# A state-space layer and a gated long convolution on one core: the same 815 operations in another order string

## The chip, the cores and the metric

The kernel runs on one core of a Trainium2 chip. The metric is the device time of one execution in microseconds (us); lower is better. TensorE is PE (its weight loads are PEld), VectorE is DVE, ScalarE is ACT, GpSimd is POOL, SyncE is SP; SPq and ACTq are the queues on which SP and ACT issue transfers.

## The reference, cut to what matters

There are two parts, each on a sequence of 2048 positions with 640 channels, and their outputs stand side by side.

```
A:  Bu   = x @ B_bar.T            (complex, 640 states)
    h_t  = Lam_bar * h_(t-1) + Bu_t
    y    = 2 * Re(h @ C.T) + x * Dskip
B:  kv   = (causal 4-tap convolution of k, by channel) * v
    y    = irfft(rfft(kv padded) * rfft(ssm_k padded))[:2048] + kv * ssm_D
    out  = q * y
result = concat([A, B], axis=-1)          # bf16, 1 x 2048 x 1280
```

## The kernel before, in words

Everything lives in one SBUF tensor (`arena`) and one PSUM tensor of eight banks (`acc`). The function `build` (it calls the methods of `PartA` and `PartB`) adds 815 small operations to a list with `P.add`. An operation has a number, a name, the engines that could run it, a function that makes its instructions, and its footprints. `depend` works out from the footprints which operation must wait for which. The string `ORDER` then says everything else: each entry is an operation's number, the letter of its engine (T PE, V DVE, A ACT, G POOL, S SP) and the first PSUM bank of its group. A small t is PE with the narrow tile form: the product is cut into two halves of the array (`wide`, L225 wide and L229 narrow; `s1`, L876 wide and L881 narrow). `emit` walks the string and makes the instructions, so each engine runs its entries in that order, and an entry that waits holds up all behind it on its engine. There is no planner in the file; only its result.

Operations of part A, in the order of the data: `warm` (L539, products that only keep PE busy at the start); `ld_Braw`, `turn_B`, `ev_B` (L517 to L526: B loaded, transposed on PE, copied out) and `ld_B2` (L512, the rest of B by transposing transfers); `ld_x` (L547, x by eight transposing transfers); `up2`, `up1`, `up0a`, `up0b`, `up0c` (L581 and L602, with evictions L598, L622, L648), a tree that combines neighbouring positions with the tables `rr` (L457, four of them, numbers 143 to 146, products on DVE); `coarse` (`cs_v`, `cs_m`, `cs_s` and so on, L666 to L690), the scan over the top of the tree in two halves, whose scratch is the buffer H0; `dn3` to `dn0` with `ad` (L225/L229 and L728), the way back down; `gm` (L457) and `gC` (L571, L575), C scaled; and `project` (L736 to L765): `ld_r`, `xd` (x times Dskip, L737), `C0` to `C15` (20 or 40 products each, L225/L229), `ev_C` (L754 on DVE, or L752 on ACT with `em_C`, L760, after it) and the store `st_A`.

Operations of part B: five blocks of 128 channels go through `ld_k`, `ld_v` (L814, transposing transfers), the convolution (`cm`, four taps, L205 on DVE and L206 on ACT; `ca`, three adds, L840; `cx`, times v, L841), a store to DRAM (`pl`, L847) and eight loads per half in another layout (`rl`, L857). There is one buffer for k, so `ld_k` of a block waits for all taps of the block before it. Two halves of the channels are then transformed: `s1` and `s2` for h (the filter, `ld_h`, L807, into H0) and for k (L876/L881 with evictions L886, and L900 with evictions L913), the complex products `pp`, `pq`, `py`, `pz` (L924 to L931), the way back `r2` (L951, L956) and `r1` (L972; L990 on DVE, or L988 on ACT and then `em1`, L995), and the stores (L1006). `c.DR` is the Dskip row spread over the partitions (`ld_Dr`, number 91, L372); `ld_D` (157 and 158, L795) are two loads of 640 bytes.

Every PSUM group takes two banks as a rule, and the group that follows on the same banks waits for the eviction of the one before. SP issues nearly all transfers, in the order of its entries.

```
order = [(int(x[:-2]), x[-2].upper(), int(x[-1])) for x in ORDER.split()] if ORDER else plain_order(c.P)
c.P.narrow = {int(x[:-2]) for x in ORDER.split() if x[-2] == "t"}
```

Of the kernel before, what the change touches and what calls it, by code (L numbers as in the profile page):

```python
# [1097 lines left out]
def plain_order(P):  # L1098
# [16 lines left out]


ORDER = (
# [40 lines left out]
)  # L1158


# [68 lines left out]
```

## Time and profile before

| what | value |
|---|---|
| median of three runs | 188.85 us (188.34 to 191.32) |
| span of the profiled execution, first to last instruction | 187.3 us |
| what lies between that span and the runs' median | 1.55 us |
| PE, DVE, ACT, POOL busy | 175.6, 158.0, 147.7, 72.6 us |
| transfers | 30.15 MB, 161 GB/s over the span |
| granted TensorE clock, mean | 0.999 |

The profiled execution's own time is known as its span; the runs' times are of whole executions. Instruction rows are start, length, engine, line, operation, output and inputs, and in brackets how long the engine idled before it and what ended that. PE's busy time counts pipelined products whose ends are modelled, so a high share is not a full array. A transfer's row on SPq is the time that its issue took, not the transfer's.

### The profile page before, as it was taken

The page shows a single profiled execution, that of the slowest core. Times are in us where ns is not written, and L with a number is a line of the kernel's source. Part 1 is how long each engine was busy: PE and PEld are TensorE (multiplying, and loading weights), DVE is VectorE, ACT ScalarE, POOL GpSimd, SP SyncE. Part 2 cuts the span into 40 slices and gives each one's busy share as a digit, 9 for nine tenths or more (in the row PEclk, how much of TensorE's full clock was granted, in tenths as well). Part 3 has the DMA queues.
Part 4 walks back from the last instruction along what each step waited for, and adds up shares of the span by engine and source line. Part 5 has one row for each costly group of instructions (what it writes and reads, how often), then busy time and mean ns, then how long its engine had stood idle before and what let it go on. Part 6 is the DMA issues. An engine that isn't in the chain of part 4 may idle for free.

```text
span 187.3 us, 7665 instructions
## 1 busy us (share of the span) xinstructions
PE 175.6 (94%) x3398; PEld 126.3 (67%) x3399; DVE 158.0 (84%) x225; ACT 147.7 (79%) x181; POOL 72.6 (39%) x68
## 2 busy tenths in 40 slices
PE   7998999999799979979997999999999999999992
PEld 2565666677468756656685688776588876887770
DVE  3537964679959899999969999899999999998961
ACT  2469699989899979999997997997898883985000
POOL 8679999900000000008803925730740000551620
PEclk9999999999999999999999999999999999999999
DMA  5999999799999989999989479402496993058996
GB/s 153 191 184 158 200 143 140 141 174 182 198 253 154 290 179 152 180 182 154 138 109 251 154 170 133 75 5 72 122 196 120 210 227 85 15 160 187 208 219 173
DMA packets 106682, 30.15 MB, mean 161 GB/s; under 512 B 101274, under 2 KB 106010, under 8 KB 106650
## 3 DMA queue, kind: packets, MB, share of 16 engines
q1 hardware_dynamic: 106332, 29.35, 86.7%
q8 instruction: 26, 0.43, 1.1%
q10 hardware_dynamic: 318, 0.33, 0.6%
q14 instruction: 6, 0.05, 0.1%
HBM read 11.32 MB, written 7.86 MB: 102 GB/s over the span
## 4 chain that ended last, share of the span: by engine, by line
PE 54%; DVE 23%; DMA 9%; ACT 8%; issue 3%; DVEq 0%; ACTq 0%
PE acc L225 17%; PE acc L581 13%; DMA arena<-in_B_k_dram 9%; PE acc L229 6%; DVE arena L728 6%; PE acc L900 6%; DVE arena L205 5%; ACT arena L913 5%; PE acc L951 4%; DVE arena L840 3%; PE acc L972 3%; PE acc L539 2%; DVE arena L754 2%; PE acc L881 1%; ACT arena L886 1%
## 5 line engine op out<-in xcount | busy, mean ns | idle before, releaser
L581 PE MATMUL acc<-arena 128*64 128x512 bf16 x400 | 45.6, 380 | 1.8 <-DVE arena L457 1.1
L913 ACT CAST arena<-acc 128x960 bf16<-128x960 f32 (+1 forms) x43 | 37.4, 916 | 4.0 <-PE acc L900 2.2
L225 PE MATMUL acc<-arena 128*128 128x320 bf16 (+2 forms) x255 | 36.4, 297 | 2.2 <-DVE arena L754 1.1
L581 PEld LDWEIGHTS <-arena 128*64 128x64 bf16 x400 | 26.0, 110 | 17.8 <-DVE arena L457 1.3
L886 ACT CAST arena<-acc 128x1024 bf16<-128x1024 f32 x37 | 35.8, 1034 | 2.1 <-PE acc L881 2.0
L225 PEld LDWEIGHTS <-arena 128*128 128x128 bf16 x256 | 23.7, 98 | 12.1 <-DVE arena L754 1.3
L841 POOL TENSOR_TENSOR arena<-arena 128x2048 bf16<-128x2048 bf16 x2 | 8.8, 4410 | 53.7 <-DVE arena L840 46.1
L900 PE MATMUL acc<-arena 128*64 128x160 bf16 x512 | 23.6, 235 | 1.8 <-DVE arena L679 1.4
L900 PEld LDWEIGHTS <-arena 128*64 128x64 bf16 x512 | 18.6, 110 | 8.3 <-ACT arena L913 2.2
L229 PE MATMUL acc<-arena 128*64 128x320 bf16 (+3 forms) x258 | 23.2, 313 | 0.5 <-DVE arena L690 0.5
L840 DVE TENSOR_TENSOR arena<-arena 128x2048 bf16<-128x2048 bf16 x14 | 17.6, 1256 | 4.5 <-ACT arena L206 4.3
L728 DVE TENSOR_TENSOR arena<-acc,arena 128x1024 bf16<-128x1024 f32 (+2 forms) x19 | 20.4, 1114 | 0.9 <-PE acc L229 0.5
L760 POOL TENSOR_TENSOR arena<-arena 128x640 bf16<-128x640 f32 x3 | 4.2, 1416 | 32.6 <-ACT arena L752 32.6
L956 ACT CAST arena<-acc 128x1024 bf16<-128x1024 f32 x16 | 15.4, 1025 | 1.7 <-PE acc L951 1.6
L229 PEld LDWEIGHTS <-arena 128*64 128x64 bf16 x258 | 13.0, 110 | 3.5 <-DVE arena L690 0.6
L876 PE MATMUL acc<-arena 128*64 128x128 bf16 x400 | 14.6, 220 | 0.2 <-ACT arena L886 0.2
L876 PEld LDWEIGHTS <-arena 128*64 128x64 bf16 x400 | 12.9, 110 | 2.4 <-ACT arena L886 0.9
L205 DVE TENSOR_SCALAR arena<-arena 128x2048 bf16<-128x2048 bf16 x15 | 11.0, 749 | 3.6 <-DMA arena<-in_B_k_dram 3.5
L754 DVE TENSOR_TENSOR arena<-acc,arena 128x640 bf16<-128x640 f32 x13 | 10.7, 820 | 3.5 <-PE acc L225 2.2
L206 ACT ACTIVATE arena<-arena 128x2048 bf16<-128x2048 bf16 (+2 forms) x10 | 11.1, 1112 | 1.5 <-DMA arena<-in_B_k_dram 1.5
L924 DVE TENSOR_TENSOR arena<-arena 128x2560 bf16<-128x2560 bf16 x8 | 11.9, 1484 | 0.1
L602 PE MATMUL acc<-arena 128*64 128x256 bf16 (+2 forms) x140 | 11.6, 291 | 0.1
(142 smaller groups left out, 284.4 us busy)
## 6 DMA issues: line engine op xcount, KB each, us to landing
out_dram<-arena SPq DMA_DIRECT2D x32, 160.0 KB, 3.3
arena<-in_B_ssm_k_dram SPq DMA_DIRECT2D x8, 320.0 KB, 6.1
kv_rows<-arena SPq DMA_DIRECT2D x5, 512.0 KB, 4.7
arena<-kv_rows SPq DMA_DIRECT2D x16, 160.0 KB, 4.0
arena<-in_A_x_dram SPq DMA_DIRECT2D x16, 160.0 KB, 3.5
arena<-in_B_q_dram SPq DMA_DIRECT2D x8, 320.0 KB, 6.3
arena<-in_A_B_im_dram ACTq DMA_DIRECT2D x1, 160.0 KB, 2.8
arena<-in_A_B_re_dram SPq DMA_DIRECT2D x1, 160.0 KB, 3.0
```

Of the source, the lines that this page charges most:

```text
L205: vm = lambda e: lambda out, in_, by: e.tensor_scalar_mul(out=out, in0=in_, scalar1=by)
L225: e.matmul(out, lhsT=lhsT, rhs=rhs, start=start, stop=stop, skip_group_check=True)
L229: e.matmul(out[half], lhsT=lhsT[:, half], rhs=rhs, start=start, stop=stop, skip_group_check=True, tile_position=(0, 64 * r))
L581: e.matmul(o[64 * r:64 * r + 64], lhsT=self.BT[j][:, r, d, :], rhs=self.XP[:, d, 2 * q:2 * q + 2], start=(d == 0), stop=(d == 4), skip_gro ...
L728: e.tensor_tensor(out=o, in0=b, in1=o, op=ALU.add)
L754: e.tensor_tensor(out=two(ys), in0=two(B)[:, :, 0:320], in1=two(ys), op=ALU.add)
L840: P.add(f"ca{d}_{j}", tt, lambda e: e.tensor_tensor(out=t1, in0=t1, in1=t2, op=ALU.add), outs=[t1], ins=[t1, t2])
L876: e.matmul(B[64 * b:64 * b + 64, 128 * i:128 * i + 128], lhsT=lh[i], rhs=F[:, b, :], start=True, stop=True, tile_position=(0, 64 * b))
L886: P.add(f"e1{what}{hf}_{u}", {PACT: act(1024), PDVE: dve(1024)}, lambda e, B: c.CP[e](out=out, in_=(B.rearrange("p (l n s k) -> p k s l n" ...
L900: e.matmul(B[64 * s:64 * s + 64, 512 * b + 160 * i:512 * b + 160 * i + 160], lhsT=c.W[:, k, 64 * b:64 * b + 64], rhs=self.AS[hf][:, k, 160 ...
L913: c.CP[e](out=out, in_=b.rearrange("p r (k j n) -> p r k j n", k=n, j=4) if nj > 1 else b.rearrange("p r (k x) -> p r k x", k=n))
L956: P.add(f"er2{hf}_{u}", {PACT: act(1024), PDVE: dve(1024)}, lambda e, B: c.CP[e](out=out, in_=B.rearrange("p (s n b) -> p b s n", s=2, n=4 ...
```

## The change

Only the string `ORDER` changes. The operations, their functions, footprints and buffers stay. The new string was counted with each transfer's length as it shows behind another one. Compared entry by entry, 72 of the 815 carry another letter; four of these only issue a small load from the other of the two queues.

```diff
-    "168A0 156G0 161S0 0V0 58G0 6T0 17G0 167A0 162S0 110G0 19V0 147G0 87V0 11G0 18V0 89A0 90S0 12G0 3T1 42G0 13V0 88S0 182S0 "
...
-    "405V0 240A6 247T2 406V0 198A0 232A4 399S0 407V0 86A0 408V0 444S0 241T6 248A2 205T0 242A6 315V0 249T2 139A0 206A0 233T4 "
-    "250A2 409V0 243T6 411S0 207T0 234A4 244A6 251T2 235T4 255T6 252A2 175V0 410S0 208A0 415S0 236A4 85A0 320V0 316V0 158S0 "
-    "447V0 301T4 256A6 313T0 446V0 302A4 318t2 257T6 319V2 314A0 309T4 448V0 258A6 311T2 414S0 310A4 259T6 299T0 416S0 321V0 "
...
-    "292A2 477T0 471A6 490T2 478V0 734S0 468T4 491A2 456S0 499T6 460V0 479T0 469A4 726t2 461V0 500A6 443V0 480A0 725V0 602S0 "
-    "462A0 524t0 727V2 532t6 522t4 730V0 731T2 728S0 525A0 454S0 463V0 739S0 533A6 472V0 464G0 523A4 503T6 732V2 366t0 504A6 "
...
+    "12G0 0V0 168S0 162A0 87V0 4T0 42G0 89S0 161A0 90S0 111G0 160G0 1T1 17G0 167A0 88S0 182S0 11G0 18V0 65V0 30G0 66V0 2T2 26G0 20V0 "
...
+    "269S0 394V0 192A6 395V0 154A0 205t2 396V0 197t4 239T6 206A2 397V0 400S0 230A0 198V4 75A0 195t2 240A6 199t0 315V0 271S0 247T4 "
...
+    "243T6 249T4 244A6 86A0 270S0 233T2 407V0 255T6 141V0 408V0 388S0 314A0 234A2 140V0 409V0 139A0 16A0 175G0 444S0 235T2 250V4 "
+    "301T0 256A6 236V2 251T4 302V0 297T2 252A4 318T4 298A2 319V4 299T0 410S0 257T6 320V0 300A0 316V0 309T2 321V0 311T4 258V6 272S0 "
...
+    "466T0 158S0 469A2 479T4 91S0 470T6 460V0 467A0 726T2 461V0 724S0 471A6 480A4 729S0 443V0 472V0 462A0 456S0 532t0 522t6 731T4 "
+    "725V0 523A6 727V2 454S0 730V0 533A0 463V0 481T2 358t6 734S0 732V4 482A2 528T0 359V6 739S0 464G0 356t4 529A0 524T2 728S0 357V4 "
...
```

The places that the prediction speaks of, one engine at a time:

| engine | before | after |
|---|---|---|
| PE, start | warm x3, turn_B1, warm, turn_B0, ..., up21_0, up21_2, up20_2, up20_0, then up20_4, up20_8, up21_8, up20_6 | warm x8, t_par, turn_B1, ..., turn_B0 x2, up21_2, up21_0, up20_0, up20_2, then up21_4, up20_6, up21_8, up20_4, up20_8 |
| DVE, `rr` | 143, 146 after alb; 144 and 145 around conv 1 and its last tap | 144, 143, then tap cm0_3, 145, ca0_2, eviction ev_up20_4, ca0_1, tap cm0_0; 146 before cx0 |
| DVE, conv 1 to conv 2 | ca1_0, cx1, taps of conv 2 | ca1_0, e1h0_4, r16, cx1, e1h0_3, taps of conv 2 |
| DVE, scan | taps cm3_2, cm3_3, cs_v0_m, ca3_2, cs_w0, cm3_1, cs_s0 | ev_up0b_4, ev_up0c_0, e2h0_12, cs_v0_m, cs_a0, cs_w0, ev_up0b_6, cs_s0, cm3_2, cm3_3 |
| `gm` (175) | DVE | POOL, its last entry before cx3 |
| SP, k2 to k3 | ld_k2, pl0, ld_v2, ld_C0, pl1, ld_k3 | ld_k2, ld_C0, ld_v2, pl1, ld_C1, pl0, ld_k3 |
| SP, Dskip | ld_k4, ld_C1, ld_r1, ld_h1 x4, ld_Dr, ld_r2, ld_v4 (ld_D 158 among the rl0, ld_r0 before ld_k4) | ld_k4, ld_h1 x4, ld_D 158, ld_Dr, ld_r0, ld_r1, ld_v4 |
| PE and DVE, `C0` and `C1` | C0 on bank 2 (narrow), s1h1 x3, C1 on bank 2; pp0 after ev_C0 | C0 on bank 2 (wide), s1h1 x2, C1 on bank 4, s2k0_14 on bank 2; pp0 before xd0 |
| PE, end | r11_16, C14, C15, r11 x2, C12, C13 | C15, r11_16, r11 x2, C12, C14, C13 |

The other letters that change: DVE instead of ACT for ev_B1 (172), js0, two cf, cm0_3, cm0_0, ev_up20_4, e1h0_3, e1h0_4, ev_up0c_0, ev_up0b_4, ev_up0b_6, ev_gC0_0, e2h0_12, e1k0_0, e1h1_2, e2k1_27, er21_1, er11_0, er11_16, ev_C11; ACT instead of DVE for one cf, ev_up20_2, ev_up21_8, e1h0_6, ev_up0b_8, ev_gC0_1, ev_gC2_0, ev_gC4_0, e2k0_8, er21_0, er21_8, ev_C9; between DVE and POOL em10_0, xd2, xd14 (to DVE) and em10_12, xd7, xd8 (to POOL); and the tile form of 16 `s1`, seven of `cs_v0` and `dn`, and C0. Four more entries with a new letter make no instruction in one of the strings, as their `ev` or `er` is on DVE.

66 rows, old and new, of the table ORDER are left out of this document.

## The prediction

> **What bounds the kernel now.** I read the page's busy table first, then busy time by stage (stretches cut where the work changes), then PE's and DVE's instructions in order of time around each idle stretch, and last SyncE's queue (SPq) of DMA issues.
>
> ```profile
> span 187.3 us, 7665 instructions
> PE 175.6 (94%) x3398; PEld 126.3 (67%) x3399; DVE 158.0 (84%) x225; ACT 147.7 (79%) x181; POOL 72.6 (39%) x68
> ```
> ```profile
> 14.00:41.00 27.00, 26.37 (x277) 17.26 (x275) 19.10 (x21) 24.53 (x27) 23.72 (x21) 1.00 1.15 157
> 41.00:66.00 25.00, 23.76 (x392) 17.11 (x386) 21.98 (x29) 23.52 (x36) 0.00 (x0) 1.00 1.12 218
> 66.00:97.00 31.00, 27.77 (x627) 20.09 (x628) 30.18 (x38) 29.51 (x39) 8.14 (x2) 1.00 1.03 153
> 97.00:128.00 31.00, 29.66 (x766) 22.51 (x765) 28.71 (x30) 27.77 (x30) 15.30 (x6) 1.00 0.63 127
> 128.00:162.00 34.00, 33.39 (x785) 25.41 (x774) 32.89 (x40) 27.53 (x33) 5.82 (x4) 1.00 0.73 143
> 162.00:187.30 25.30, 21.60 (x512) 16.88 (x508) 18.83 (x22) 8.14 (x9) 9.30 (x6) 0.99 0.71 178
> ```
> The columns are stretch, length, then busy time of PE, PEld, DVE, ACT, POOL, the granted clock and DMA. Up to 41 us PE is the bound: it idles 0.6 us, while DVE has 7.9 us free (27.00 - 19.10). From 66 to 97 the two engines that empty PSUM are the bound: DVE idles 0.8 us, ACT 1.5, PE 3.2. From 97 to 128 PE idles 1.3, DVE 2.3; from 128 to 162 both are full. The granted clock is 1.00 in all but the last stretch, so the clock takes no part. PE's idle time has few places, and each goes back to something late:
>
> ```profile
> 18.65 6.67 PE L581 MATMUL acc<-arena 128*64 128x512 bf16 x60 [0.63 <-DVE arena L420]
> ```
> ```profile
> 48.06 1.48 DVE L457 TENSOR_TENSOR arena<-arena 128x1280 bf16<-128x1280 bf16 x1
> 48.12 2.13 PE L581 MATMUL acc<-arena 128*64 128x512 bf16 x18 [1.15 <-DVE arena L457]
> ```
> ```profile
> 65.20 1.42 DVE L205 TENSOR_SCALAR arena<-arena 128x2048 bf16<-128x2048 bf16 x2 [0.65 <-DMA arena<-in_B_k_dram]
> 66.53 0.82 DVE L679 TENSOR_TENSOR arena<-acc,arena 128x640 bf16<-128x640 f32 x1
> 67.41 0.61 PE L900 MATMUL acc<-arena 128*64 128x160 bf16 x12 [1.39 <-DVE arena L679]
> ```
> ```profile
> 97.87 0.49 DVE L737 TENSOR_TENSOR arena<-arena 128x640 bf16<-128x640 bf16 x1 [1.38 <-DMA arena<-in_A_Dskip_dram]
> 98.49 0.82 DVE L754 TENSOR_TENSOR arena<-acc,arena 128x640 bf16<-128x640 f32 x1
> 99.37 0.85 PE L225 MATMUL acc<-arena 128*128 128x320 bf16 x5 [0.97 <-DVE arena L754]
> ```
> The reader is to see four waits. At 18.65 the fifth `up2` starts late. At 48.12 `up0a_2` lacks the second `rr` table (144), which stands behind conv 1 on DVE. At 67.41 `s2h0_24` needs the banks of `cs_v0`, whose multiply stands on DVE behind two taps of conv 3, and those wait for k3's transfer. At 99.37 `C1` needs the banks of `C0`, emptied only after `xd0`, which waits for the Dskip row.
>
> **Part by part.** *The work.* The 815 entries are the same; 72 have another letter. By form, DVE gains and loses PSUM evictions so: 1024 columns 6 in, 5 out; 960 columns 4 in, 1 out; 640 columns 2 in, 4 out; 256 columns 3 in, 1 out. It gains two taps of conv 0, and `gm` goes from DVE to POOL.
>
> ```profile
> L886 DVE CAST arena<-acc 128x1024 bf16<-128x1024 f32 x3 | 3.6, 1215 | 0.0
> L913 DVE CAST arena<-acc 128x960 bf16<-128x960 f32 x3 | 3.5, 1154 | 0.0
> L575 DVE CAST arena<-acc 128x640 bf16<-128x640 f32 x4 | 3.3, 815 | 0.0
> L648 DVE CAST arena<-acc 128x256 bf16<-128x256 f32 x1 | 0.4, 448 | 0.0
> L205 DVE TENSOR_SCALAR arena<-arena 128x2048 bf16<-128x2048 bf16 x15 | 11.0, 749 | 3.6 <-DMA arena<-in_B_k_dram 3.5
> L206 ACT ACTIVATE arena<-arena 128x2048 bf16<-128x2048 bf16 x5 | 10.0, 2006 | 1.5 <-DMA arena<-in_B_k_dram 1.5
> L927 POOL TENSOR_TENSOR arena<-arena 128x1280 bf16<-128x1280 bf16 x2 | 5.2, 2616 | 6.8 <-DVE arena L924 3.4 <-PE acc L900 3.4
> ```
> DVE: +1.22 + 3 x 1.15 - 2 x 0.82 + 2 x 0.45 + 2 x 0.75 - 1.48 (`gm`, by the L457 row) = +4.0; one eviction of `turn_B1` on DVE (between 0.4 and 0.8 by the L648 and L575 rows, taken at 0.8, the same columns) and one 640-column product gone to POOL (-0.5, by the `xd0` row at 97.87) make it +4.3. ACT loses two taps, -4.0, and more evictions than it takes. PE's products stay: 16 `s1` operations change tile form, 9 to narrow and 7 to wide, and 8 smaller ones, which cancels nearly: 0. POOL takes `gm`; it has no row for that broadcast, the nearest is 2.6 us, and POOL does nothing from 41 to 66 us (0.00). If `gm` came late, `gC` would wait. Its last input stands behind conv 2's adds, about 60 us (k3's issue at 59.81, below, follows the last tap of conv 2); its first reader stands on PE behind `cs_k0`, which needs a scan that follows `cs_v0`'s multiply at 66.53, or some 2 us sooner. So 0, and 2.6 if that cover goes.
>
> What covers DVE's +4.3 is its own idle time, which the trace puts in front of late inputs:
>
> ```profile
> 32.33 1.45 DVE L840 TENSOR_TENSOR arena<-arena 128x2048 bf16<-128x2048 bf16 x1 [2.52 <-ACT arena L206]
> 37.89 1.23 DVE L841 TENSOR_TENSOR arena<-arena 128x2048 bf16<-128x2048 bf16 x1 [1.83 <-DMA arena<-in_B_v_dram]
> 41.15 1.42 DVE L205 TENSOR_SCALAR arena<-arena 128x2048 bf16<-128x2048 bf16 x2 [0.90 <-DMA arena<-in_B_k_dram]
> 53.96 0.75 DVE L205 TENSOR_SCALAR arena<-arena 128x2048 bf16<-128x2048 bf16 x1 [1.90 <-DMA arena<-in_B_k_dram]
> ```
> These are 7.2 us. The new queue puts all four `rr`, both taps and an eviction ahead of conv 1 (before 41 us), and `e1h0_4`, `r16`, `e1h0_3` in front of k2's taps. So I count 0 for the load, and +4.3 where the cover fails.
>
> *The start.* Both queues run four `up2` of 2.2 us first (6.67 for three in the 18.65 row) and then one that needs the transposed B (ld_B2), whose second half is the 11.88 issue below; four before, five after 18.65. The new order starts with eight warm-ups and finishes its B turns some 0.3 us later, which this wait swallows. 0; bounds -0.6 and +0.3.
>
> *The `rr` wait.* `rr` 144 now runs before `rr` 143, well ahead of its reader: -1.15.
>
> *The `cs_v0` wait.* Its multiply now precedes the k3 taps: -1.39. What is late next there is k3, and its taps then follow the scan.
>
> ```profile
> 11.88 2.52 SPq L512 DMA_TRANSPOSE arena<-in_A_B_im_dram  x1
> 34.99 2.69 SPq L814 DMA_TRANSPOSE arena<-in_B_k_dram  x1
> 48.18 2.14 SPq L814 DMA_TRANSPOSE arena<-in_B_k_dram  x1
> 59.81 3.06 SPq L814 DMA_TRANSPOSE arena<-in_B_k_dram  x1
> 64.74 1.61 SPq L795 DMA_DIRECT2D arena<-in_B_ssm_D_dram  x1
> 82.93 7.61 SPq L807 DMA_DIRECT2D arena<-in_B_ssm_k_dram  x4
> 90.58 3.45 SPq L372 DMA_DIRECT2D arena<-in_A_Dskip_dram  x1
> ```
> SPq issues end to end from the 11.88 row to the end of the 59.81 row, 22 issues, so k1 and k2 keep their times whatever DVE does. k3 is moved behind one more C transpose (at most 3.1, as the 59.81 row's), but DVE now has the scan chain ahead of its taps: 0.
>
> *The Dskip row.* The four h1 loads must still wait for `cs_h1`, which leaves their buffer; behind them now stands the second ld_D as well, and only then Dskip and the two x rows. ld_D took 1.61 us, 1.4 of it a wait:
>
> ```profile
> SPq L795 <- ACT arena L913: 1.4, 1, 1.4
> ```
> ```profile
> 178.06 5.55 PE acc L225 x40
> ```
> ```profile
> 100.77 1.48 DVE L924 TENSOR_TENSOR arena<-arena 128x2560 bf16<-128x2560 bf16 x1
> ```
> So Dskip lands 0.2 us later (bounds 0 and 1.6). But `C1` is on banks of its own now (4, where it was 2), and PE runs its 2.8 us (half of the 5.55 for two projections) before it blocks on `s2k0_14`. On PE's side the 2.54 us of the two waits survive less 0.2: -2.3. On DVE's side, from `ev_C0` to `ev_C4`, one eviction and one `xd` come in (1.2 + 0.5) and one `pp0` goes out in front (1.5), so the work is the same to within 0.2 us, and DVE can give no more than its free 2.29 us in this stage less the 1.38 of the wait itself: -0.9 + 0.2 = -0.7. The stage is between the two, PE slightly fuller (29.66 of 31.00 against 28.71): I take -1.5.
>
> *The end.* PE ends with projections, two before and three after (`C14` has changed places with two `r11`), and the last eviction is the same: 0.
>
> **Sum:** 0 for the start, -1.15, -1.39, and 1.04 given back at the Dskip row: -1.5 us against the span of 187.3, so 185.8. The three runs' median of 188.85 lies 1.55 above that span, which I carry over: 187.4 us, range of this case 186.5 to 188.2 (from -2.3 and -0.7).
>
> *POOL beside DVE.* The first two `rr` ran while POOL multiplied, the others did not:
>
> ```profile
> 18.66 3.74 DVE L457 TENSOR_TENSOR arena<-arena 128x1280 bf16<-128x1280 bf16 x2
> 19.19 1.86 POOL L309 TENSOR_TENSOR arena<-arena 128x512 int32<-128x512 int32 x1
> ```
> Two took 3.74 us, where two alone (the 48.06 row) take 2.96. Two more `rr` move into that time: +0.8 on DVE, inside its 7.9 free microseconds, so 0 in the sum and 0.8 without cover. The Trainium skill, "GPSIMD Engine Reference", section 1 "Specifications", says that GpSimd shares its SBUF interfaces with VectorE and that they contend when the DVE instruction has two SBUF inputs. The trace agrees, with the 3.74; by that rule `gm` on POOL, beside conv 2's adds, would also stretch DVE, and the slow case below would be some 0.8 us dearer.
>
> **Rivals.** *A, all late inputs are met:* if the transfers fit the new order as a whole, PE's idle from 41 to 128 goes (1.24 + 3.23 + 1.34 = 5.8): 183.0. For it: PE has the work, and ACT is relieved. Against: DVE idles 0.8 us from 66 to 97, so the evictions must shift to ACT there, and ACT has 1.5.
>
> *B, the transfers decide and have not moved:* k1, k2, h1 and Dskip are tied to SPq and to `cs_h1`; whatever is saved ahead of them is waited out: 188.9. For it: the unbroken SPq. Against: two of the four waits are not transfers' alone.
>
> *C, slower: DVE becomes the bound from 41 us on.* Its place is the stages from 41 to 162, where DVE has 0.8 to 3.0 us free; its price is the whole +4.3: 193.2. It decides as soon as less than 4.3 of the idle 7.2 us before 54 us is filled with the moved work, since DVE's free time later (2.3 and 1.1) is already in the sum. For it: `e1k0_0`, `e1h1_2` and `e2k1_27` go to DVE in its full stages. Against: three `gC` evictions and `e2k0_8` leave it there.
>
> **How the numbers follow.** Forecast 0.36, A 0.26, B 0.21, C 0.17. Two per cent, about what a measurement of this kernel can tell from no change, is 185.1 and 192.6. Faster: A and a little of the forecast's lower side, 0.29. Slower: most of C and a little of B, 0.17. Within: 0.54. The range goes from 182.4, which is A with the start's 0.6 gone too, to 193.0, nearly C's full price; it holds the 1.6 of Dskip and the 2.6 of `gm`.
>
> **What would show it.** Right: PE's idle before `up0a_2` and before the `s2` behind `cs_v0` is under 0.3 us; k1's and k2's issues stay within 1 us of 34.99 and 48.18; DVE still waits over 1 us for Dskip near 98 us; PE is full from 128 us to the end. Wrong: k1 or k2 issued over 2 us earlier, or `xd0` without a wait (then A); DVE over 98% busy from 41 to 162 with PE idling longer than 5.8 us from 41 to 128 (then C); a new wait of POOL's `gm` before `gC`.

## The result, and the profile after

The kernel after takes 189.16 us (median of 18 runs, 187.76 to 190.79), the kernel before 188.84 beside it (18 runs): ratio 1.0055, 95% interval 1.0029 to 1.0080. That is about 1.0 us slower, where the forecast said 1.5 us faster, and no change by the 2% measure. Ratios throughout are to the kernel before on the same chip and leave out runs over 1.5% above their kernel's fastest: here seven of the kernel before's 18 and one of the other 18 (with them the medians differ by 0.32 us), the profiles of e7 and e9, and that of e18 but for the wait at 48 us. By either count the forecast's gain is not there; that the kernel is slower rests on the ratio. The profiled execution of the kernel after took 188.45 us, 1.75 more than its span.

The page's first lines and the busy times by stage (columns as before):

```profile
span 186.7 us, 7677 instructions
PE 175.3 (94%) x3409; PEld 123.5 (66%) x3409; DVE 169.3 (91%) x232; ACT 139.5 (75%) x172; POOL 75.2 (40%) x68
```
```profile
14.00:41.00 27.00, 25.92 (x300) 16.23 (x297) 25.27 (x26) 21.71 (x22) 26.23 (x21) 1.00 1.15 172
41.00:66.00 25.00, 24.37 (x492) 16.23 (x490) 23.67 (x29) 22.07 (x33) 3.22 (x1) 1.00 1.12 196
66.00:97.00 31.00, 28.09 (x558) 19.54 (x557) 29.70 (x39) 29.67 (x39) 8.14 (x2) 1.00 1.17 162
97.00:128.00 31.00, 30.07 (x775) 23.18 (x774) 29.92 (x33) 26.97 (x30) 13.77 (x5) 1.00 0.88 176
```
DVE is busy 11.3 us longer, not 4.3, and 6.2 of it lie in the first stage, where it now has 1.7 us free instead of 7.9. PE's idle time has new places. The view of PE's waits (us in total, times, longest), then four PE rows:

```profile
PE acc L876 <- ACT arena L886: 1.4, 4, 0.6
PE acc L876 <- DMA arena<-kv_rows: 1.2, 1, 1.2
PE acc L581 <- DMA arena<-in_A_B_im_dram: 1.1, 1, 1.1
```
```profile
19.46 0.84 PE L581 MATMUL acc<-arena 128*64 128x512 bf16 x6 [1.08 <-DMA arena<-in_A_B_im_dram]
48.09 1.27 PE L581 MATMUL acc<-arena 128*64 128x512 bf16 x10
66.02 1.41 PE L900 MATMUL acc<-arena 128*64 128x160 bf16 x36
97.61 2.89 PE L225 MATMUL acc<-arena 128*128 128x320 bf16 x20
```
`up0a_2` (48.09), the `s2` behind `cs_v0` (66.02) and `C1` (97.61) start without their waits of 1.15, 1.39 and 0.97 us. All three waits are gone, and the kernel is not faster. In their place the fifth `up2` waits 1.08 us for B, and the first `s1k0` 1.2 us for its rows from DRAM, then four times for evictions of its own kind. DVE's rows up to k2, POOL's products beside the first of them, and on SPq the k loads with what stands ahead of them (start, length):

```profile
20.39 3.75 DVE L457 TENSOR_TENSOR arena<-arena 128x1280 bf16<-128x1280 bf16 x2
25.50 2.33 DVE L457 TENSOR_TENSOR arena<-arena 128x1280 bf16<-128x1280 bf16 x1
27.75 2.06 DVE L840 TENSOR_TENSOR arena<-arena 128x2048 bf16<-128x2048 bf16 x1
29.73 1.21 DVE L598 CAST arena<-acc 128x1024 bf16<-128x1024 f32 x1
33.89 1.34 DVE L205 TENSOR_SCALAR arena<-arena 128x2048 bf16<-128x2048 bf16 x1
...
39.21 2.54 DVE L457 TENSOR_TENSOR arena<-arena 128x1280 bf16<-128x1280 bf16 x1
...
47.68 0.76 DVE L205 TENSOR_SCALAR arena<-arena 128x2048 bf16<-128x2048 bf16 x1
```
```profile
22.75 7.96 POOL L309 TENSOR_TENSOR arena<-arena 128x512 int32<-128x512 int32 x4
```
```profile
30.08 4.81 SPq L814 DMA_TRANSPOSE arena<-in_B_v_dram  x1
35.30 2.29 SPq L814 DMA_TRANSPOSE arena<-in_B_k_dram  x1
...
43.87 3.14 SPq L556 DMA_TRANSPOSE arena<-in_A_C_re_dram  x1
48.46 2.43 SPq L814 DMA_TRANSPOSE arena<-in_B_k_dram  x1
...
58.91 1.79 SPq L556 DMA_TRANSPOSE arena<-in_A_C_re_dram  x1
...
61.44 3.37 SPq L814 DMA_TRANSPOSE arena<-in_B_k_dram  x1
```
k1 is issued when conv 0's last tap ends (33.89 + 1.34 = 35.23), k2 when conv 1's ends (47.68 + 0.76 = 48.44): DVE holds both. SPq itself was free from 34.89 (the end of v0's row) and 47.01 (of the C row), so DVE's own part is 0.3 us of k1 and 1.4 us of k2. k3 waits for SPq's own queue, the moved C1 load (58.91) in it.

### The profile page after: what moved, and what is told of

Its sections match the earlier page's. It is cut to its first block, busy times and chain, and to the rows that moved or that the text cites. A ratio compares the mean times of both kernels' runs of the same rounds, so it can differ in the third digit from the quotient of the medians.

```text
span 186.7 us, 7677 instructions
## 1 busy us (share of the span) xinstructions
PE 175.3 (94%) x3409; PEld 123.5 (66%) x3409; DVE 169.3 (91%) x232; ACT 139.5 (75%) x172; POOL 75.2 (40%) x68
## 4 chain that ended last, share of the span: by engine, by line
PE 62%; ACT 12%; SPq 10%; DVE 6%; DMA 6%; issue 2%; ACTq 0%; DVEq 0%
PE acc L225 19%; PE acc L581 18%; ACT arena L913 5%; ACT arena L886 5%; PE acc L229 4%; PE acc L900 4%; SPq L547 4%; PE acc L876 4%; PE acc L602 4%; SPq L857 4%; PE acc L951 4%; DMA arena<-in_A_B_im_dram 4%; DVE arena L728 3%; PE acc L972 3%; DMA arena<-kv_rows 2%
## 5 line engine op out<-in xcount | busy, mean ns | idle before, releaser
L225 PE MATMUL acc<-arena 128*128 128x320 bf16 (+2 forms) x278 | 40.8, 300 | 0.2
L913 ACT CAST arena<-acc 128x960 bf16<-128x960 f32 (+1 forms) x42 | 36.1, 912 | 4.2 <-PE acc L900 2.2
L581 PEld LDWEIGHTS <-arena 128*64 128x64 bf16 x400 | 25.1, 110 | 18.0 <-issue 2.6
L886 ACT CAST arena<-acc 128x1024 bf16<-128x1024 f32 x34 | 32.7, 1032 | 1.9 <-PE acc L876 1.2
L225 PEld LDWEIGHTS <-arena 128*128 128x128 bf16 x278 | 25.8, 98 | 11.0 <-ACT arena L956 0.4
L900 PEld LDWEIGHTS <-arena 128*64 128x64 bf16 x512 | 18.6, 110 | 7.1 <-ACT arena L913 2.5
L840 DVE TENSOR_TENSOR arena<-arena 128x2048 bf16<-128x2048 bf16 x14 | 18.6, 1330 | 1.2 <-ACT arena L206 0.9
L229 PE MATMUL acc<-arena 128*64 128x320 bf16 (+3 forms) x214 | 19.1, 308 | 0.1
L956 ACT CAST arena<-acc 128x1024 bf16<-128x1024 f32 x17 | 16.3, 1027 | 2.7 <-PE acc L951 2.6
L876 PE MATMUL acc<-arena 128*64 128x128 bf16 x368 | 13.4, 220 | 2.7 <-ACT arena L886 1.4
L205 DVE TENSOR_SCALAR arena<-arena 128x2048 bf16<-128x2048 bf16 (+2 forms) x19 | 14.8, 796 | 0.8 <-DMA arena<-in_B_k_dram 0.3
L876 PEld LDWEIGHTS <-arena 128*64 128x64 bf16 x368 | 11.3, 110 | 5.7 <-ACT arena L886 3.0
L309 POOL TENSOR_TENSOR arena<-arena 128x512 int32<-128x512 int32 x8 | 12.8, 1623 | 0.1
L229 PEld LDWEIGHTS <-arena 128*64 128x64 bf16 x214 | 10.6, 110 | 2.5 <-ACT arena L913 0.5
L602 PE MATMUL acc<-arena 128*64 128x256 bf16 (+2 forms) x140 | 11.7, 292 | 0.6 <-DVE arena L648 0.6
```

Source lines behind the costliest of these rows:

```text
L205: vm = lambda e: lambda out, in_, by: e.tensor_scalar_mul(out=out, in0=in_, scalar1=by)
L225: e.matmul(out, lhsT=lhsT, rhs=rhs, start=start, stop=stop, skip_group_check=True)
L229: e.matmul(out[half], lhsT=lhsT[:, half], rhs=rhs, start=start, stop=stop, skip_group_check=True, tile_position=(0, 64 * r))
L581: e.matmul(o[64 * r:64 * r + 64], lhsT=self.BT[j][:, r, d, :], rhs=self.XP[:, d, 2 * q:2 * q + 2], start=(d == 0), stop=(d == 4), skip_gro ...
L602: e.matmul(o[64 * r:64 * r + 64], lhsT=self.c.RR[:, n, j, 64 * r:64 * r + 64], rhs=x, start=False, stop=True, skip_group_check=True, tile_ ...
L840: P.add(f"ca{d}_{j}", tt, lambda e: e.tensor_tensor(out=t1, in0=t1, in1=t2, op=ALU.add), outs=[t1], ins=[t1, t2])
```

## The experiments

Diffs show the entries of one engine; the rest of the string stays. The theories are named in the expectations: F the forecast's reasons; E the evicting engines bind from 66 us; R and S the relay of k, v and rows through the transfers; D DVE's queue; L the first loads; C the rival of that letter; P PE's own work.

### Is a wait won when it is taken away?

**e1_rr**, `rr` 144 early (DVE):
```diff
-131V0 143V0 146V0 129V0 ... 396V0 144V0 135V0
+131V0 144V0 143V0 146V0 129V0 ... 396V0 135V0
```


> The kernel before with one DVE entry moved: rr 144 directly ahead of rr 143. Three theories. F (the forecast): a wait of PE that is taken away is won, so PE's 1.15 us before up0a_2 at 48.12 goes and the time falls by 1.15 us, ratio 0.994. E (evictions bind): from 66 to 97 us DVE and ACT are busy 59.7 of 62 us, so what PE wins ahead of 66 us is waited out there unless DVE and ACT get to start earlier; ACT has 1.5 us free there, so 0 to -0.5 us, ratio 0.997 to 1.000, and C0 still starts within 0.5 us of 94.5. R (the relay of loads): the loads of this kernel do not move, s1k0 stays at 77.1 us, so 0 us, ratio 1.000.


**e2_scan**, the scan's multiply ahead of conv 3's taps (DVE):
```diff
-316V0 447V0 446V0 319V2 448V0
+316V0 319V2 447V0 446V0 448V0
```


> The kernel before with one DVE entry moved: the multiply of cs_v0 (319) ahead of conv 3's first tap (447), which waits for k3. F: PE's 1.39 us before the s2 at 67.41 goes and the time falls by 1.39 us, ratio 0.993. E: the idle of PE at this place shrinks to under 0.5 us but comes back as waits for banks before 97 us; C0 starts within 0.4 us of 94.5 and the time is the same within 0.4 us, ratio 0.998 to 1.002. R: the same as E in the time, but the wait that comes back is the one of s1k0 for its rows from DRAM near 77 us.


**e3_c1**, C1 on its own banks (PE):
```diff
-524t0 532t6 522t4 731T2 503T6
+524t0 532t6 731T4 522t2 503T6
```


> The kernel before with C1 ahead of s1h1_4 on PE and the two groups' banks exchanged (C1 on bank 4, s1h1_4 on bank 2). F: PE's 0.97 us before C1 goes and 1.0 us is won of the time, ratio 0.994. E: the same place has DVE with 2.3 us free and PE with 1.3 in the stage from 97 to 128 us, so up to 1 us may be won by C3 (109.48) and about half of it at the end, ratio 0.997. R says nothing of this place: ratio 0.994 to 1.000.


Measured: 1.0012 (0.9980 to 1.0044), 1.0022 (0.9984 to 1.0060), 0.9999 (0.9962 to 1.0037). F's 0.994, 0.993 and 0.994 lie below all three intervals, and E's times are inside. (For C1, F goes further than the forecast, whose sum gives 1.04 us back at the Dskip row and wins nothing there.) And the profile of e3, whose entries are the kernel before's up to C0, shows no wait before `up0a_2` and only 0.3 us behind `cs_v0`. So the kernel before was profiled again, and all three edits were made at once.

**e15_same**, no edit, and **e13_three**, the three diffs above together:

> The kernel before, unchanged, for a second profile of it. P: the transfers' lengths differ from one execution to the next, so PE's waits differ too: the wait for rr 144 at 48 us and the one for cs_v0's multiply at 67 us are under 0.5 us, PE idles 2.4 to 3 us from the fifth up2 to C0 instead of 4.5; the ratio is 1.000. F: both waits are there again, within 0.3 us of 1.15 and 1.39.

> The kernel before with all three edits of the forecast's sum at once: rr 144 first, the multiply of cs_v0 ahead of conv 3's taps, C1 on banks of its own. F: -1.15 - 1.39 - 1.04 = -3.6 us, ratio 0.981. P: those waits were those of one execution; in three other executions of the same entries PE idles 2.4 to 2.8 us from the fifth up2 to C0, not 4.5, so there is little left to remove: PE idles 2.0 to 2.8 us there and 1.5 to 2.5 behind it, ratio 0.995 to 1.002.


e15: 0.9997 (0.9962 to 1.0032). Its rows at the three places, and the `rr` behind conv 1:
```profile
46.67 2.35 PE L581 MATMUL acc<-arena 128*64 128x512 bf16 x20
...
65.75 0.60 PE L900 MATMUL acc<-arena 128*64 128x160 bf16 x12 [0.81 <-DVE arena L679]
...
97.66 2.89 PE L225 MATMUL acc<-arena 128*128 128x320 bf16 x20 [0.91 <-DVE arena L754]
```
```profile
44.46 1.49 DVE L457 TENSOR_TENSOR arena<-arena 128x1280 bf16<-128x1280 bf16 x1
```
The same string, another execution: the first wait is not there, the second is 0.81 instead of 1.39, only the third is the same. `rr` 144 runs at 44.46, not 46.58, because k1 was issued earlier. The load of v0 ahead of it, first in the kernel before's first profile, then in e15, with k1 behind it there:
```profile
29.80 5.08 SPq L814 DMA_TRANSPOSE arena<-in_B_v_dram  x1
```
```profile
29.57 3.99 SPq L814 DMA_TRANSPOSE arena<-in_B_v_dram  x1
33.66 2.52 SPq L814 DMA_TRANSPOSE arena<-in_B_k_dram  x1
```
The same issue took 5.08 us once and 3.99 the other time. Five more profiles have the same entries up to there. In e2, e3, e16 and e17 v0's issue took 3.88 to 4.13 us, and `up0a_2` does not wait for `rr`; in e18 it took 5.15, and the wait is back:
```profile
29.94 5.15 SPq L814 DMA_TRANSPOSE arena<-in_B_v_dram  x1
```
```profile
PE acc L581 <- DVE arena L457: 1.1, 1, 1.1
```
The wait of 1.15 us goes with a late transfer, two executions in seven.

e13: 1.0088 (1.0052 to 1.0125), slower; F's 0.981, and the 0.992 of the forecast's own sum, are not there. Its profiled execution is the fastest of its nine (187.99 us) and ends as e15's does; so it does not show the whole loss, but it shows where each gain goes. DVE, then PE:
```profile
18.59 5.99 DVE L457 TENSOR_TENSOR arena<-arena 128x1280 bf16<-128x1280 bf16 x3
...
33.27 2.08 DVE L840 TENSOR_TENSOR arena<-arena 128x2048 bf16<-128x2048 bf16 x1 [2.07 <-ACT arena L206]
```
```profile
73.38 0.47 PE L571 MATMUL acc<-arena 64*64 64x320 bf16 x8 [0.67 <-DVE arena L679]
```
Three `rr` beside POOL take 5.99 us (two took 3.74), conv 0 and its evictions end some 1.5 us later, and `up0a_2` starts at 47.69, 1.07 us *later* than in e15 (0.32 of it from the start; 47.77 in e1), to save a wait that was not there. The scan's edit wins 0.56 us against e15 by 67 us; then conv 3's taps stand ahead of the scan's next multiply, `gC` waits for its banks (0.67), and 0.95 is lost by 73 us. C1's edit wins 0.89 by 100 us, and 0.43 is given back by 104.

### A ledger of PE

From the fifth `up2` to the last of the late projections, C13, PE's busy time is 155.5 to 157.2 us in every profile read. I cut the windows view at the fifth `up2`, C0 and C13 (first weight loads) and took idle as length less PE's busy time; rows of the kernel before, of e15, of the kernel after and of e5:
```profile
18.62:94.52 75.90, 71.41 (x1211) 50.02 (x1214) 65.67 (x82) 70.67 (x89) 27.24 (x18) 1.00 1.12 177
94.52:180.59 86.07, 84.12 (x2052) 64.96 (x2047) 80.71 (x91) 65.92 (x74) 30.00 (x15) 1.00 0.68 143
```
```profile
18.51:92.87 74.36, 71.44 (x1212) 50.18 (x1214) 66.03 (x82) 70.52 (x89) 28.37 (x19) 1.00 1.15 181
92.87:179.49 86.62, 84.02 (x2051) 64.81 (x2046) 80.75 (x91) 65.96 (x74) 30.06 (x15) 1.00 0.70 143
```
```profile
19.43:94.14 74.71, 71.15 (x1276) 47.53 (x1277) 70.67 (x80) 68.25 (x87) 32.25 (x19) 1.00 1.15 175
94.14:180.15 86.01, 84.46 (x1993) 64.97 (x1992) 82.12 (x93) 63.01 (x71) 27.77 (x14) 1.00 0.69 149
```
```profile
19.28:92.71 73.43, 70.99 (x1274) 47.63 (x1276) 69.74 (x79) 67.96 (x87) 30.79 (x19) 1.00 1.10 179
```

| profile | ratio | fifth `up2` | PE busy | idle to C0 | idle C0 to C13 | C13 |
|---|---|---|---|---|---|---|
| before, first | | 18.62 | 155.5 | 4.49 | 1.95 | 180.59 |
| before, second (e15) | 0.9997 | 18.51 | 155.5 | 2.92 | 2.60 | 179.49 |
| e1 | 1.0012 | 18.80 | 156.4 | 2.54 | 2.11 | 179.82 |
| e2 | 1.0022 | 18.65 | 156.0 | 2.84 | 2.03 | 179.48 |
| e3 | 0.9999 | 18.16 | 155.9 | 2.44 | 2.96 | 179.42 |
| e13 | 1.0088 | 18.83 | 156.5 | 3.16 | 1.18 | 179.68 |
| e6 | 0.9946 | 18.66 | 155.7 | 2.41 | 1.49 | 178.23 |
| after | 1.0055 | 19.43 | 155.6 | 3.56 | 1.55 | 180.15 |
| e4 | 1.0091 | 19.20 | 156.5 | 4.11 | 2.03 | 181.83 |
| e5 | 1.0017 | 19.28 | 155.5 | 2.44 | 1.89 | 179.15 |
| e8 | 1.0158 | 18.96 | 155.8 | 5.03 | 1.54 | 181.29 |
| e10 | 1.0206 | 19.18 | 156.1 | 4.48 | 1.58 | 181.31 |
| e11 | 1.0170 | 19.12 | 156.2 | 4.53 | 1.96 | 181.81 |
| e12 | 1.0102 | 19.09 | 156.1 | 2.16 | 1.87 | 179.21 |
| e14 | 1.0205 | 18.85 | 157.2 | 3.51 | 2.57 | 182.12 |
| e16 | 0.9967 | 18.83 | 155.5 | 3.71 | 1.72 | 179.77 |
| e17 | 0.9975 | 18.81 | 155.6 | 3.04 | 1.46 | 178.90 |

C13 is the fifth `up2` plus work plus idle, so between these two points an order string can win no more than the idle, 3.9 to 6.6 us. The idle to C0 varies by itself: before, e15 and e3 have the same entries up to C0, and 4.49, 2.92 and 2.44 us. A difference of up to 2 us between two profiles there can be chance. Against e15 the kernel after has 0.92 (start) + 0.15 (busy) + 0.64 (to C0) - 1.05 (behind C0) = +0.66 us, an account of these two executions. The spans differ by 0.7, the many runs by 1.0.

### Do the transfers set the end?

**e4_loads** (SP; `gC4`'s two products go behind 437 and 490 on PE):
```diff
-400S0 271S0 401S0 399S0 270S0 388S0 444S0 410S0 272S0 417S0 ... 416S0 445S0 455S0
+400S0 388S0 271S0 401S0 399S0 444S0 410S0 417S0 ... 416S0 272S0 445S0 455S0 270S0
```


> The kernel after with the loads of k2 to k4 on SP as in the kernel before: pl0 directly behind ld_k2, one ld_C1 behind the eight rl0, the other behind ld_k4; and, since gC4 needs them, its two products and evictions placed as before (behind s1k0_9 and s2k0_19). R: k3 is issued near 59.8 instead of 61.44 and s1k0_2 starts near 77.1 instead of 79.85; the time falls by 1 to 2.5 us against the kernel after, ratio to the kernel before 0.992 to 1.000. E: s1k0 starts earlier too, but e1k0_9 still ends its wait within 0.5 us of 87.8 and C0 starts within 0.5 us of 94.1, ratio to before 1.003 to 1.008 as the kernel after has it.


1.0091 (1.0049 to 1.0133). `s1k0_2` starts 1.07 us earlier and C0 1.07 later: `gC4`, taken out of the time before `s1k0`, stands behind it now, and PE waits 1.1 us ahead of its second product (at 92.00). R falls.

**e6_less_load**, a load left out of the kernel before:
```diff
-            if o.group is None:
+            if i == 269:
+                pass
+            elif o.group is None:
```


> The kernel before without the first ld_C0 (269), the transposing load between ld_v1 and ld_k2; it leaves out this part of C, so the first output is computed with old data there. S: SPq has 3.1 us less ahead of k2; k2 then follows conv 1's last tap, 1.2 to 1.5 us after where SPq allowed it before, k3 comes 1.5 to 2.6 us earlier, s1k0_2 and C0 (17.4 us behind it in the kernel before and in three of its variants) too, and the time falls by 1.5 to 2.5 us, ratio 0.987 to 0.992. E: the loads are not what sets C0; ratio 0.997 to 1.002.


0.9946 (0.9916 to 0.9976): 1.0 us of the 1.5 to 2.5. Against e15, k3 comes 2.2 us earlier, the first `s1k0` only 0.37, since PE arrives there by its own work. Behind C0, with Dskip issued at 88.03 instead of 89.20, idle is 1.1 us less. The kernel lacks what that load brings, so this prices the load and is no faster kernel: transfers matter, but not one for one.

**e7_half_first** and **e8_both** (SP; `s1k0` and `gC` permuted to suit):
```diff
-272S0 417S0 415S0 411S0 418S0 413S0 414S0 412S0 416S0
+272S0 411S0 412S0 413S0 414S0 415S0 416S0 417S0 418S0
```


> The kernel after with the eight rl0 in the order of their use (first the four that s1k0_0 to s1k0_4 read, then the four of s1k0_5 to s1k0_9) and the ten s1k0 in the order 2, 3, 1, 4, 0, 5, 6, 8, 7, 9 on the same places, banks and engines. S: the last row that s1k0_2 needs is issued four loads earlier, so the 1.2 us that PE waited for kv_rows goes; s1k0_2 starts at 78.5 (PE's own work) instead of 79.85 and the time falls by 1.0 to 1.3 us, ratio to before 0.999. E: s1k0_2 starts at 78.5 too, but its evictions wait behind the ones of gC and s2h0, C0 starts within 0.4 us of 94.1, ratio 1.003 to 1.008.


```diff
-270S0 388S0 444S0 410S0 272S0 417S0 ...
+388S0 270S0 411S0 412S0 444S0 410S0 413S0 414S0 272S0 415S0 ...
```


> The kernel after with both: rr 146 behind ca1_0; on SP two of the first four rl0 ahead of k3, the other two directly behind pl2, then ld_C1 (272) and the other four; s1k0 in the order of their rows; the two gC4 products last but one among gC, since their load is later. S: k2 near 47.2, s1k0's rows complete by 75 us, PE reaches s1k0_2 at 77 without a wait and the time falls by 2 to 2.9 us (2.9 is all that PE idles from 66 to 97 us in the kernel after), ratio to before 0.990 to 0.995, the fastest of all. E: DVE and ACT together have 2.6 us free of 62 from 66 to 97 us, so at most half of that, 1.3 us, ratio 0.998 to 1.003.


e7: 1.0003 (0.9959 to 1.0048), undecided between S and the kernel after. e8: 1.0158 (1.0101 to 1.0215). The wait for the rows is gone, but the two rows ahead of k3 waited 1.3 us for their store, k3 was issued at 64.03, conv 3's taps came late, and the scan's multiply stands behind them; e8's longest PE wait:
```profile
PE acc L571 <- DVE arena L679: 2.1, 2, 1.9
```
That is the prediction's `cs_v0` wait again, one scan step on.

**e9_first_loads**, the loads up to k1 as before (SP; 168, 167, 89 on ACT):
```diff
-168S0 89S0 90S0 88S0 182S0 ... 174S0 378S0 155S0 184S0 178S0 179S0 157S0 185S0 187S0 186S0 379S0
+161S0 162S0 90S0 88S0 182S0 ... 174S0 155S0 378S0 178S0 187S0 179S0 186S0 185S0 157S0 184S0 379S0
```


> The kernel after with all loads up to ld_k1 on the queues and in the order of the kernel before (161, 162, 90, 88 first on SP, 168, 167, 89 on ACT; then sk, k0, x2, h0, x3, h0, h0, D, h0, v0, k1). L (the first loads): in four executions of the kernel before and its variants ld_B2's second half is issued at 11.5 to 12.0 and the fifth up2 starts at 18.2 to 18.8; in five of the kernel after and its variants at 12.3 to 12.8 and 18.9 to 19.4. If the order of the first loads does that, the fifth up2 starts near 18.6, all of PE's work is 0.6 us sooner and the time falls by 0.6 us, ratio to before 1.002. D (DVE's queue holds k1 and k2 back): k1 is still issued right behind conv 0's last tap, 35.0 to 35.3, k2 at 48.1 to 48.5, and the ratio stays at 1.004 to 1.007.


1.0063 (1.0022 to 1.0104): nothing won. Three more kernels with these loads (e10 to e12) issue the second half of B at 11.5 to 11.7, as before, and start the fifth `up2` at 19.1 to 19.2 all the same. L's gain is not there. In all 17 profiles read, the start lies 4.2 to 4.9 us behind the end of that issue. In strings from after the start is late (18.85 to 19.43 against 18.16 to 18.83). With their own first loads the issue is late too, at 12.3 to 12.8; e10 to e12 issue it early, but it takes 2.7 to 3.3 us there (1.75 to 2.6 in strings from before). What decides its length and its landing stays open.

### Is it DVE?

**e5_rr_late** (DVE):
```diff
-386V0 146V0 387V0 64V0 ... 397V0 198V4
+386V0 387V0 64V0 ... 397V0 146V0 198V4
```


> The kernel after with one DVE entry moved: rr 146 behind ca1_0, out of the way of cx0 and conv 1's taps. S (the chain of k loads and the relay through DRAM set C0's start, and in the kernel after DVE holds k2 back): k2 is issued at the end of SPq's own work, 47.0 to 47.5 instead of 48.46, k3 at 60.1 instead of 61.44, s1k0_2 starts 1.0 to 1.4 us earlier than 79.85, and the time falls by as much, ratio to the kernel before 0.998. E (from 66 us the two evicting engines set C0's start): k2 and k3 move as said, C0 still starts within 0.4 us of 94.1 and the ratio stays at 1.003 to 1.008.


1.0017 (0.9980 to 1.0055). k2 goes at 46.78 and k3 at 59.76, 1.7 us earlier each, and C0 starts 1.43 us earlier, as S says. That one `rr` held back k2 is shown: conv 1's last tap ends at 46.5 to 47.1 in e5, e8, e12 and e14, which have it late, and at 48.4 to 48.5 in the kernel after and e4. The gain in time is not shown: the interval overlaps that of the kernel after, and C0 alone moves by more between executions of the same entries (94.52, 92.87 and 92.02 in before, e15 and e3).

**e12_loads_rr**, e9's and e5's diffs together:

> The kernel after with two edits together: the loads up to ld_k1 as in the kernel before (as in e9_first_loads) and rr 146 behind ca1_0 (as in e5_rr_late). P (PE's own work decides: from the fifth up2 to C13 PE has 155.5 to 156.5 us of work in every kernel profiled so far, and the time is the fifth up2's start, that work, and PE's idle time): the fifth up2 starts near 18.5 as in e9_first_loads and PE idles near 2.4 us to C0 as in e5_rr_late; C0 at 92.0, ratio to before 0.995 to 0.999. If the two do not add, PE's idle grows by what the start gains: ratio 1.001 to 1.006.


1.0102 (1.0050 to 1.0153). They do not add. The profiled execution, the fastest of its six, idles least of all to C0 (2.16), and the others are slower; open.

**e10_taps**, on e9: DVE's `rr` 145 and 146 late, two evictions back on ACT, and on ACT a tap earlier:
```diff
-70A0 153A0 216A2 63A0 383A0
+70A0 383A0 153A0 216A2 63A0
```


> The kernel of the run before this one, and on DVE rr 145 and 146 behind ca1_0, r16 behind ca2_0, on ACT the tap cm0_1 ahead of a sine, and e1h0_3 and e1h0_4 on ACT again. D: conv 0's last tap ends near 32.7 instead of 35.2, so k1 is issued when SPq is free, 33.4 to 34.0, k2 at 45.5 to 46.6, k3 at 58 to 59.5, s1k0_2 at 76.5 to 78; with the 14.3 us from there to C0 that the kernel after and e5_rr_late have, C0 starts at 91 to 92.3 and the time falls by 1.5 to 2 us against the kernel after, ratio to before 0.994 to 0.998. L alone: 1.002.


1.0206 (1.0147 to 1.0266). Conv 0's last tap ends at 33.0, as D wants, but k1 goes only at 34.48: the tap on ACT also stands ahead of the sine (63) that v0's load waits for, and v0's issue slides to 32.10. And the tap now stands ahead of `ev_up20_6`, which starts at 30.69 instead of 27.72, and PE pays at once:
```profile
PE acc L581 <- ACT arena L598: 1.5, 1, 1.5
```
PE is 1.7 us late at `up1_6`, and C13 is 1.16 us late. **e11_all** adds e7's diff, and its first `s1k0` starts where e10's does (80.90 against 80.89):

> The kernel of the run before this one, and the eight rl0 and ten s1k0 in the order of their use, as in e7_half_first. D with the relay: PE no longer waits for kv_rows at the first s1k0, which starts with PE's own work, 0.5 to 1.2 us earlier than in the run before this one; ratio to before 0.988 to 0.994. If DVE and ACT bind from 66 to 97 us, s1k0 starts earlier and C0 does not: ratio as in the run before this one within 0.003.


1.0170 (1.0112 to 1.0229).

**e14_evict**, on e5, six evictions by letter:
```diff
-198V4 196V2 302V0 420V6 519V4 666V4
+198A4 196A2 302A0 420A6 519A4 666A4
```


> The kernel of e5_rr_late with six evictions that the change put on DVE on ACT again: e1h0_3, e1h0_4, e2h0_12, e1k0_0, e1h1_2, e2k1_27, 7 us less on DVE. C (DVE is the bound from 41 us on): the time falls by 1 us or more against e5_rr_late, ratio to before under 0.997. P: DVE's load matters only where PE waits for it; ACT is as full as DVE from 66 to 97 us, so PE's idle to C0 stays at 2.4 to 3.2 us, ratio 0.999 to 1.006.


1.0205 (1.0164 to 1.0246): moving 7 us of evictions from DVE to ACT costs 2%. C's gain is not there; PE waits for ACT instead (the first row is not in e5, the second is 0.9 us there):
```profile
PE acc L900 <- ACT arena L886: 1.1, 3, 0.6
PE acc L876 <- ACT arena L886: 1.1, 4, 0.3
```

### The wait that is in both profiles

**e16_dskip** (SP; measured again as **e18_dskip_again**) and **e17_dskip_c1**, the same with e3's diff:
```diff
-158S0 414S0 ... 439S0 91S0 734S0
+158S0 91S0 414S0 ... 439S0 734S0
```


> The kernel before with one SP entry moved: ld_Dr directly behind ld_D 158, where SP idles 1.3 us until the row store of block 2 has landed. P: DVE's wait for Dskip ahead of xd0 goes (1.38 and 0.70 us in the two profiles of the kernel before), ev_C0 and C1 start 0.7 us earlier; the third wait of the forecast is the only one that is in both profiles. If nothing else is late there, PE's idle from C0 to C13 falls from 2.0 to 2.6 us to about 1.3 and the ratio is 0.995 to 0.997; if it is given back as in e3_c1 and e13_three, the ratio is 0.999 to 1.003.

> The kernel before with ld_Dr early as in the run before this one and C1 on banks of its own as in e3_c1: the whole of the forecast's third term (DVE's wait and PE's). F: -1.0 to -2.3 us, ratio 0.988 to 0.995. P: no more than the Dskip row alone gives, ratio 0.995 to 1.002.

> The kernel of e16_dskip once more, for a narrower interval: 0.9967 with 0.9926 to 1.0007 the first time. If the early Dskip row wins what it did there, 0.994 to 0.999; if that was chance, 0.999 to 1.003.


0.9967 (0.9926 to 1.0007), 0.9980 (0.9941 to 1.0019) and 0.9975 (0.9943 to 1.0007). All three are below 1 and each interval holds 1: some 0.5 us, not told apart from nothing one by one. All three lie below the kernel after's interval. e17 lies above F's 0.988 to 0.995, though its interval reaches into it. PE's idle from C0 to C13 is 1.72 (e16) and 1.46 us (e17). What is late next in e16 is h1:
```profile
96.49 0.53 DVE L809 TENSOR_TENSOR arena<-arena 128x80 bf16<-128x80 bf16 x1 [1.00 <-DMA arena<-in_B_ssm_k_dram]
```

## Why the prediction was wrong, step by step

- **The sum's two largest terms, -1.15 (`rr`) and -1.39 (`cs_v0`), are the steps that failed.** Both waits were read from one profile as if the program had them. In a second profile they are 0 and 0.81 us; removed one by one they give nothing, and removed together (with C1 on its own banks) they cost 0.9%. The first comes with a v0 issue of over 5 us, which makes k1 late, and its price was charged to DVE's order. The second moves to the scan's next multiply, as e2, e13 and e8 show.
- **"So I count 0 for the load" failed too.** The list of entries gave +4.3; DVE's busy time grew by 11.3. The moved entries come to 7.2 us instead of 4.3 (the two taps beside POOL 1.4 dearer, and `js0`, 0.9, was not in the list), and entries that stayed take 4.8 more, less 0.7 that overlaps. The +0.8 for contention was the mis-sized term: of the two `rr` in 3.74 us the first took 1.49 and the second 2.33. Up to 41 us 1.7 us are free instead of 7.9, and DVE then holds k1 and k2.
- **"k1 and k2 keep their times whatever DVE does"**: they are within 1 us of the first profile's, as forecast, but for another reason. In the second profile they go at 33.66 and 46.64, so after they are 1.6 and 1.8 us later. Of k1's 1.6, 1.3 is SPq's own (v0 is issued 0.5 later and takes 0.8 longer) and 0.3 DVE's, but DVE alone is enough: in e12 SPq is free at 33.98, and k1 still goes at 35.34. Of k2's, 1.4 is DVE's, and e5 gets it back.
- **k3 at 0** was wrong: 61.44 against 59.81 and 58.27, and the first `s1k0` waits 1.2 us for rows behind it.
- **The start at 0**, bounds -0.6 and +0.3: the fifth `up2` is 0.8 to 0.9 us later, outside the bounds. It waits for the second half of B, whose issue starts at 12.60 and ends at 15.08, not 11.88 and 14.40; the sum left that issue where it was.
- **The Dskip row**: the forecast kept DVE's wait of over 1 us near 98; there is none, since DVE has `pp0` in front of it. C1 starts 1.8 us earlier than in the first profile (97.61 against 99.37; 97.66 in the second), and C2 0.2 later (115.20 against 115.02): given back in between.
- **`gm` at 0** was right: 3.2 us on POOL (the 41 to 66 row) instead of the nearest row's 2.6, with no wait of `gC` for it. Nor did it stretch DVE, as the prediction's slow case has it: conv 2's product with v, two SBUF inputs, took 1.23 us beside it (at 61.91). **The end at 0** was right: 6.55 us from C13 to the last instruction against 6.7 and 6.5. From C0 to C13, where the forecast gave 1.04 us back, it is 86.01 against 86.07 and 86.62.
- **The rivals.** A falls with the waits. B came nearest in time (188.9); its reason holds in part, as e6 shows. C was wrong in place as far as the runs show: DVE's load holds the k chain before 48 us; from there on, e14 takes 7 us of it away, gives it to ACT and loses 2%.

What stays open: whether the kernel after is slower or only not faster, what sets the landing of B's second half, and why e12 and e13 are slower in most runs than their profiled execution shows.

## What to carry to other kernels

Profile the kernel before more than once before pricing a wait: one that hangs on a transfer's length may be absent from the next execution. Price a moved operation by what it costs where it goes, not where it was. Where one engine's work is nearly the whole span, keep a ledger of start, work and idle: a removed wait counts only if idle falls up to a point far behind it.

## What was not expected of the hardware

- One string, two executions: the issue of v0 took 5.08 and 3.99 us, and C0 started at 94.52 and 92.87. Over seven executions it took 3.88 to 4.13 us five times and over 5 us twice.
- Beside POOL's products, DVE's `rr` take 2.33 us instead of 1.49, 2048-column adds 2.06 instead of 1.22, and taps, which read one SBUF tensor, 1.34 to 1.53 instead of 0.75. The eviction from PSUM at 29.73, among them, keeps its 1.21. POOL's L309 products grow too, from 1.14 us in the mean to 1.62. In e5, moved to 47.93 where POOL does nothing, `rr` 146 takes 1.49 us instead of 2.54. The Trainium skill, "GPSIMD Engine Reference", section 1 "Specifications", names contention for DVE instructions in a two-port mode or with two SBUF inputs; the rows agree for `rr` and the adds, which have two SBUF inputs, and add the size; beside `gm` a product with two kept its 1.23. Whether the taps run in such a mode no run here shows.
